# A four-byte read of every later w1 row, placed behind the first x load

## The chip, the core and the metric

The kernel runs on one core of a Trainium2 chip. The metric is the device time of one execution in microseconds, given as the median of several runs. The profile is of one execution, and its times count from the first instruction of its span.

## What is computed

The reference is a two-layer network with a SiLU between, and its gradients:

```
h   = x @ w1            x: 2048 x 640, w1: 640 x 1536
out = silu(h) @ w2      w2: 1536 x 640
(out, dx, dw1, dw2) for the given grad_out, through jax.vjp
```

All tensors are bfloat16. The outputs are out, the gradient of x, that of w1 and that of w2.

## The kernel before

Sizes in the code: S = 2048 rows of x, D = 640, F = 1536, P = 128 partitions, so DT = 5 slices of D and FT = 12 blocks of F. The rows of x are taken in NCH = 4 chunks of SC = 512.

For each chunk the kernel forms h transposed (F on the partitions) from w1 and the transposed x. ScalarE makes the activation aT, ScalarE and VectorE together make its derivative, and g_group (L296 to L308) multiplies that by the gradient that comes back through w2. Two calls of sd_phase (L310 to L328) make the chunk's out and gradient of x. After the four chunks two loops (L398, L425) make the gradients of w2 and of w1.

The first chunk is arranged apart, because nothing is on the chip yet. The names that matter for the change:

- L156 to L160: VectorE fills a 128 x 128 tile, warm, and TensorE multiplies it by itself NWARM = 18 times while the first loads are under way.
- load_x (L182) loads 128 rows of x, 1,280 bytes a row. Block 0 goes out on SP's queue and block 1 on ACT's (L188).
- load_w1 (L185) loads slice k of w1, 128 rows, one to a partition. Slice 0 goes in two halves of columns: columns 0 to 767 on SP, 768 to 1535 on ACT (L189), 1,536 bytes a row each. Slices 1 to 4 go on SP, 3,072 bytes a row (L190 to L192). The tile is w1_nat; the profile's names leave its number out and show it as w_nat, as they do for w2_nat, and show w1 and w2 as in_w_dram.
- L193: SP then transposes the other half of the chunk (rows 256 to 511 of x) on the way in. Behind it on SP's queue stand w2 (L196), the transposed gradient goT (L197, issued at L177), the transposed w2 (L199) and the transposed w1 (L200).
- The list early names the instructions that start_before_entry_wait (L16) moves ahead of the wait at the program's entry: the warm-up, the two x loads, slice 0 and slices 1 and 2. An engine's instructions in that list keep their order.
- pe_x (L202) transposes the first 256 rows of x on TensorE (L208); VectorE and ScalarE copy the result into xT (L213).
- h_first (L268) goes over the slices of w1 first: for each of the 5 slices, 6 pairs of blocks of 256 columns of F are multiplied with the first 256 rows of x (h_pair_mm, L246), two products a pair, so 12 products a slice and 60 in all. Pairs 0 to 2 use the first half of slice 0, pairs 3 to 5 the second half. Then the other 256 rows follow, pair by pair, 60 products more, and sd_phase with w2_nat begins.

[...]Tile contexts put in the semaphore waits. A DMA signals completion on one of eight semaphores, which are used in turn; a DMA that takes a semaphore again waits until its former DMA has landed.

Of the kernel before, what the change touches and what calls it, by code (L numbers as in the profile page):

```python
# [75 lines left out]
def kernel(  # L76
# [11 lines left out]
    nc = tc.nc  # L88
    P = 128
# [8 lines left out]
    ST, DT, FT = S // P, D // P, F // P  # L98
# [11 lines left out]
    dt_in = x.dtype  # L110
# [15 lines left out]
    w1_v = w1.rearrange("(dt p) f -> p dt f", p=P)  # L126
# [19 lines left out]
    with ExitStack() as mctx:  # L146
        cpool = mctx.enter_context(tc.tile_pool(name="cpool", bufs=1))
# [6 lines left out]

        warm = cpool.tile([P, P], dt_in, name="warm")
        early = [nc.vector.memset(warm[:], 1.0)]  # L156
        warm_a = cpool.tile([P, 1], FP32, name="warm_a")
        wp = ps_h.tile([P, SC], FP32, name="wp", tag="hp")
        for i in range(NWARM):
# [22 lines left out]
        def load_x(eng, q):  # L182
            return eng.dma_start(out=x_nat[:, q, :], in_=x_v[:, q, :])  # L183

        def load_w1(k, cols=slice(0, F), eng=nc.sync):  # L185
            return eng.dma_start(out=w1_nat[:, k, cols], in_=w1_v[:, k, cols])

        early += [load_x(nc.sync, 0), load_x(nc.scalar, 1)]  # L188
        early += [load_w1(0, slice(0, F // 2)), load_w1(0, slice(F // 2, F), nc.scalar)]  # L189
        early += [load_w1(k) for k in range(1, 3)]  # L190
        for k in range(3, DT):
# [138 lines left out]
        for c in range(NCH):  # L330
# [15 lines left out]
            if c == 0:  # L346
                h_first(xT, aT, ghT)
                nc.sync.dma_start(
                    out=aT_scr[:, c * SC:(c + 1) * SC].rearrange("(ft p) s -> p ft s", p=P), in_=aT[:]
                )  # L350
                sd_phase(c, w2_nat, aT, oT_scr)
                for ft in range(FT):
                    g_group(ft, goT, ghT)
                nc.sync.dma_start(
                    out=ghT_scr[:, c * SC:(c + 1) * SC].rearrange("(ft p) s -> p ft s", p=P), in_=ghT[:]
# [4 lines left out]
            for i in range(FT + LAG):  # L360
# [7 lines left out]
                out=aT_scr[:, c * SC:(c + 1) * SC].rearrange("(ft p) s -> p ft s", p=P), in_=aT[:]  # L368
            )
            nc.sync.dma_start(  # L370
                out=ghT_scr[:, c * SC:(c + 1) * SC].rearrange("(ft p) s -> p ft s", p=P), in_=ghT[:]
# [7 lines left out]
    with ExitStack() as fctx:  # L379
# [45 lines left out]
        for fc in range(NFC):  # L425
            gh_blk = gh_blks[fc]
            for dt_ in range(DT):
                if dt_ == DT // 2:
                    store_gw2(fc)
                if fc == NFC - 1 and dt_ == DT - 1:  # L430
                    last_stores = []
                    for k, (lo, hi) in enumerate(((0, FC - P), (FC - P, FC))):
# [12 lines left out]
                        else:  # L445
                            nc.vector.tensor_copy(out=g1[:, lo:hi], in_=gp[:, lo:hi])  # L446
                        store = nc.sync.dma_start(
                            out=gw1_v[:, dt_, fc * FC + lo:fc * FC + hi], in_=g1[:, lo:hi]
# [50 lines left out]
```

## Time and profile before

| | us |
|---|---|
| median of 6 runs | 321.42 |
| lowest and highest | 320.25, 322.51 |
| the profiled execution's own time | 322.51 |
| its span, first to last instruction | 320.7 |
| TensorE busy in the span | 315.6 (98%) |
| VectorE busy, ScalarE busy | 102.8, 76.8 |
| bytes moved by DMA | 67.02 MB, 209 GB/s in the mean |

An instruction is shown with the line that made it, its engine, what it writes and reads, and its busy time. An engine name with a q (SPq, ACTq, PEq) is the engine's sequencer, which issues transfers and waits. Matmuls are pipelined: one is shown with its full length from issue to last write, and the distance from one start to the next says what it costs in a row. The time from a DMA's issue to its landing is given apart from the time that its issue takes.

### The profile page before, as it was taken

What the parts mean: (1) busy time and instruction counts of PE and PEld (TensorE: products, weight loads), DVE (VectorE), ACT (ScalarE), POOL (GpSimd) and SP (SyncE); (2) the same over time, 40 slices, a digit from 0 to 9 for tenths busy, and PEclk for the clock granted to TensorE, in tenths of its full rate; (3) what the DMA queues carried; (4) which work ended last, traced back from release to release, by engine and by line L of the source; (5) the groups of instructions that cost most, each with busy time, mean ns of one, the idle gap of its engine ahead of it and who ended that gap; (6) DMA issues with size and microseconds to landing.
All of it is one profiled execution on the core that took longest, in us unless ns stands there. A gap on an engine that the chain in (4) does not pass through costs nothing.

```text
span 320.7 us, 3632 instructions
## 1 busy us (share of the span) xinstructions
PE 315.6 (98%) x1516; PEld 151.7 (47%) x1544; DVE 102.8 (32%) x182; ACT 76.8 (24%) x139; POOL 0.7 (0%) x6
## 2 busy tenths in 40 slices
PE   8999999999999999999999999999999999999997
PEld 6864444444444444444444444444444444444444
DVE  1387450377511077720047751000000110001001
ACT  2392001454211165401145520110100001001010
POOL 0000000000000000000000000000000000000000
PEclk9999999999999999999999999999999999999999
DMA  8999999999969876191636069909999999996111
GB/s 274 302 177 211 211 273 247 325 277 303 293 164 346 213 223 168 57 342 46 174 124 165 0 220 272 246 7 293 213 256 268 243 204 338 243 296 215 47 35 49
DMA packets 147232, 67.02 MB, mean 209 GB/s; under 512 B 113936, under 2 KB 146704, under 8 KB 147216
## 3 DMA queue, kind: packets, MB, share of 16 engines
q1 hardware_dynamic: 146928, 66.43, 82.0%
q10 hardware_dynamic: 288, 0.36, 0.3%
q8 instruction: 12, 0.20, 0.3%
q14 instruction: 4, 0.03, 0.0%
HBM read 9.18 MB, written 28.97 MB: 119 GB/s over the span
## 4 chain that ended last, share of the span: by engine, by line
PE 97%; DMA 2%; issue 1%; ACTq 0%; DVE 0%; DVEq 0%
PE hp L315 32%; PE hp L299 16%; PE hp L404 16%; PE hp L455 15%; PE hp L217 12%; PE hp L246 4%; DMA w_nat<-in_w_dram 2%; PE hp L435 1%; ACTq L183 0%; DVE g L446 0%; DVEq L446 0%; ACTq L483 0%
## 5 line engine op out<-in xcount | busy, mean ns | idle before, releaser
L299 PE MATMUL hp<-goT,w2T 128*128 128x512 bf16 x239 | 56.8, 379 | 0.1
L315 PE MATMUL hp<-ghT,w1T 128*128 128x512 bf16 x235 | 52.2, 379 | 0.3
L315 PE MATMUL hp<-aT,w_nat 128*128 128x512 bf16 x234 | 52.1, 379 | 0.3
L404 PE MATMUL hp<-a_blk,go_nat 128*128 128x512 bf16 x235 | 51.7, 379 | 0.3
L455 PE MATMUL hp<-gh_blk,x_nat 128*128 128x512 bf16 x219 | 48.2, 379 | 0.3
L217 PE MATMUL hp<-xT,w_nat 128*128 128x512 bf16 x174 | 43.4, 379 | 0.3
L323 ACT ACTIVATE oT<-hp 128x512 bf16<-128x512 f32 x24 | 14.5, 604 | 106.8 <-PE hp L315 106.8
L299 PEld LDWEIGHTS <-w2T 128*128 128x128 bf16 x240 | 23.5, 98 | 28.3
L404 PEld LDWEIGHTS <-go_nat 128*128 128x128 bf16 x240 | 23.5, 98 | 28.3
L315 PEld LDWEIGHTS <-w1T 128*128 128x128 bf16 x240 | 23.4, 97 | 28.4
L315 PEld LDWEIGHTS <-w_nat 128*128 128x128 bf16 x240 | 23.5, 98 | 28.1
L306 DVE SCALAR_TENSOR_TENSOR ghT<-ghT,hp 128x512 bf16<-128x512 bf16 x48 | 32.5, 682 | 7.3 <-PE hp L299 7.3
L455 PEld LDWEIGHTS <-x_nat 128*128 128x128 bf16 x224 | 21.9, 98 | 26.4
L325 DVE CAST oT<-hp 128x512 bf16<-128x512 f32 x16 | 11.1, 692 | 72.2 <-PE hp L315 67.7
L226 ACT ACTIVATE aT<-hp 128x512 bf16<-128x512 f32 x36 | 21.5, 597 | 30.4 <-PE hp L217 30.4
L217 PEld LDWEIGHTS <-w_nat 128*128 128x128 bf16 x180 | 17.6, 98 | 21.2
L233 DVE SCALAR_TENSOR_TENSOR ghT<-aT,v 128x512 bf16<-128x512 bf16 x36 | 24.7, 686 | 0.2
L232 DVE TENSOR_SCALAR v<-t 128x512 bf16<-128x512 f32 x36 | 15.4, 427 | 26.7 <-ACT t L230 26.7
L230 ACT ACTIVATE t<-hp 128x512 f32<-128x512 f32 x36 | 21.3, 591 | 0.0
L466 DVE CAST g<-hp 128x512 bf16<-128x512 f32 x7 | 4.8, 692 | 47.0 <-PE hp L455 27.7
L414 DVE CAST g2T<-hp 128x512 bf16<-128x512 f32 x7 | 4.8, 692 | 46.1 <-PE hp L404 46.1
L246 PE MATMUL hp<-xT,w_nat 128*128 128x256 bf16 x120 | 15.9, 301 | 0.6 <-DMA w_nat<-in_w_dram 0.6
(28 smaller groups left out, 68.5 us busy)
## 6 DMA issues: line engine op xcount, KB each, us to landing
aT_scr<-aT SPq DMA_DIRECT2D x4, 1536.0 KB, 6.3
ghT_scr<-ghT SPq DMA_DIRECT2D x4, 1536.0 KB, 8.2
out_dram<-o_sb SPq DMA_DIRECT2D x8, 640.0 KB, 3.3
oT_scr<-oT SPq DMA_DIRECT2D x4, 640.0 KB, 3.6
go_nat<-in_grad_out_dram SPq DMA_DIRECT2D x4, 640.0 KB, 7.4
gxT_scr<-oT SPq DMA_DIRECT2D x4, 640.0 KB, 4.7
w_nat<-in_w_dram SPq DMA_DIRECT2D x1, 1920.0 KB, 11.2
x_nat<-in_x_dram SPq DMA_DIRECT2D x3, 640.0 KB, 7.1
```

Of the source, the lines that this page charges most:

```text
L217: nc.tensor.matmul(hp[:], lhsT=w1_nat[:, dt_, ft * P:(ft + 1) * P], rhs=xT[:, dt_, :], start=(dt_ == 0), stop=(dt_ == DT - 1),)
L226: nc.scalar.activation(aT[:, ft, :], hp[:], ACT.Silu)
L230: nc.scalar.activation(t[:], hp[:], ACT.Tanh, scale=0.5)
L232: nc.vector.tensor_scalar(out=v[:], in0=t[:], scalar1=-0.5, scalar2=0.5, op0=ALU.mult, op1=ALU.add)
L233: nc.vector.scalar_tensor_tensor(out=ghT[:, ft, :], in0=aT[:, ft, :], scalar=1.0, in1=v[:], op0=ALU.subtract, op1=ALU.mult)
L246: nc.tensor.matmul(hp[:, q, :], lhsT=w1_nat[:, dt_, ft * P:(ft + 1) * P], rhs=xT[:, dt_, cols], start=(dt_ == 0 and q == qs[0]), stop=(dt_ ...
L299: nc.tensor.matmul(gp[:], lhsT=w2T[:, dt_, ft * P:(ft + 1) * P], rhs=goT[:, dt_, :], start=(dt_ == 0), stop=(dt_ == DT - 1),)
L306: nc.vector.scalar_tensor_tensor(out=ghT[:, ft, :], in0=ghT[:, ft, :], scalar=1.0, in1=gp[:], op0=ALU.add, op1=ALU.mult)
L315: nc.tensor.matmul(op_[:], lhsT=w_all[:, ft, dt_ * P:(dt_ + 1) * P], rhs=rhs_all[:, ft, :], start=(ft == 0), stop=(ft == FT - 1),)
L323: nc.scalar.activation(oT[:, dt_, :], op_[:], ACT.Copy)
L404: nc.tensor.matmul(gp[:], lhsT=go_nat[:, st, dt_ * P:(dt_ + 1) * P], rhs=a_blk[:, st, :], start=(st == 0), stop=(st == ST - 1),)
L455: nc.tensor.matmul(gp[:], lhsT=x_nat[:, st, dt_ * P:(dt_ + 1) * P], rhs=gh_blk[:, st, :], start=(st == 0), stop=(st == ST - 1),)
```

## The change

A tile of 128 x 4 x 2 elements is added, and one DMA on SP's queue right behind block 0 of x. It reads the first two elements (4 bytes) of each row of w1 in slices 1 to 4: 512 rows, four to a partition. Row p of a slice goes to partition p, as it does in load_w1. The DMA joins the list early. Nothing reads the tile.

```diff
         warm = cpool.tile([P, P], dt_in, name="warm")
         early = [nc.vector.memset(warm[:], 1.0)]
+        touch = cpool.tile([P, DT - 1, 2], dt_in, name="touch")
         warm_a = cpool.tile([P, 1], FP32, name="warm_a")
...
         early += [load_x(nc.sync, 0), load_x(nc.scalar, 1)]
+        early += [nc.sync.dma_start(out=touch[:], in_=w1_v[:, 1:DT, 0:2])]
         early += [load_w1(0, slice(0, F // 2)), load_w1(0, slice(F // 2, F), nc.scalar)]
         early += [load_w1(k) for k in range(1, 3)]
         for k in range(3, DT):
```

## The prediction

> **What bounds the kernel now.** I read the chain that ended last, then the waits of the first 14 us, then the same stretch in order of time.
>
> ```profile
> PE 97%; DMA 2%; issue 1%; ACTq 0%; DVE 0%; DVEq 0%
> PE hp L315 32%; PE hp L299 16%; PE hp L404 16%; PE hp L455 15%; PE hp L217 12%; PE hp L246 4%; DMA w_nat<-in_w_dram 2%; PE hp L435 1%; ACTq L183 0%; DVE g L446 0%; DVEq L446 0%; ACTq L483 0%
> ```
>
> TensorE carries 97% of the chain; the only load on it is w1 (w_nat), 2%. So only the start can move, and a shift there reaches the end one to one if nothing later is waited for. The chain cut to its first 16 us names the load:
>
> ```profile
> 0.63 5.46 DMA w_nat<-in_w_dram
> 6.08 0.04 issue
> 6.13 9.95 PE hp L246 x73
> ```
>
> The transfer issued at 0.63 us (columns 768 to 1535 of slice 0, from ACT) landed at 6.08 and released the products at 6.13. The stretch in order of time (start, length, what, idle before):
>
> ```profile
> 0.54 2.31 SPq L186 DMA_DIRECT2D w_nat<-in_w_dram  x5
> 0.63 0.45 ACTq L186 DMA_DIRECT2D w_nat<-in_w_dram  x1
> 2.84 1.25 PE L208 MATMUL tp<-ident,x_nat 128*128 128x128 bf16 x10 [0.23 <-DMA x_nat<-in_x_dram]
> 3.22 3.67 SPq L193 DMA_TRANSPOSE xT<-in_x_dram  x1
> 3.70 0.85 DVE L213 COPY xT<-tp 128x256 bf16<-128x256 bf16 x2 [3.24 <-PE tp L208]
> 4.04 1.44 PE L246 MATMUL hp<-xT,w_nat 128*128 128x256 bf16 x6
> 6.13 6.13 PE L246 MATMUL hp<-xT,w_nat 128*128 128x256 bf16 x38 [0.65 <-DMA w_nat<-in_w_dram]
> ```
>
> Six products run from 4.04, then TensorE stands for 0.65 us, and from 6.13 it never stops in this stretch. The same products do not always cost the same (stretch, busy, instructions):
>
> ```profile
> 6.13:9.73 3.60, 3.60 (x18) 2.54 (x18) 1.00 1.09 266
> 9.91:13.95 4.04, 4.04 (x39) 3.63 (x37) 1.00 1.10 343
> ```
>
> Their starts lie 213 ns apart until about 9.8 us and 109 ns apart afterwards. The PEclk column prints 1.00 all along; the spacing shows that the array ran at half speed before.
>
> When each slice landed, from the trace's landing records (first of the 16 DMA engines to last, us): slice 0 first half (SP) 3.00 to 3.84; second half (ACT) 3.67 to 6.08; slice 1 4.68 to 6.98; slice 2 5.83 to 7.97; slice 3 7.04 to 8.90; slice 4 9.79 to 9.86. Slice 1 is as late as the half before it: its six products end at 6.13 + 6 x 0.2135 = 7.41, and slice 1 came at 6.98. Some engines trail by about 2 us. The packet records say why: a 3,072-byte row takes 121 ns in the median, but between 3.3 and 5.7 us rows of 1.32 and 1.64 us occur, and some twenty over 0.2 us; later rows hardly ever. This is what a touch could act on.
>
> [...]The profile names no engines, but each w1 landing shows 16 increments. [...]unbroken work from 6.13, full speed at about 9.87, 3.74 us later.[...]
>
> **The change, part by part.**
>
> *SP issue.* One more DMA at 0.54. A 128-row w1 load takes 0.42 us to issue and the next one starts 0.46 after it; w2's 1,536 rows at L196 take 0.58. 512 rows lie between: I take 0.46 (0.42 to 0.65). It pushes slice 0's first half and slices 1 to 4.
>
> *A lane.* The waits of SP show that the ninth DMA waits for an x load before it reuses its semaphore:
>
> ```profile
> SPq L193 <- DMA x_nat<-in_x_dram: 0.3, 1, 0.3
> ```
>
> With one DMA more, the ninth is slice 4, not xT's transpose. It then goes out at about 3.2 instead of 2.43; behind it wait the xT transpose (3.22 to some 3.7), w2_nat and goT. Slice 4 is needed when 48 products have passed: six to 5.27, 18 from 6.13 cold to about 9.9, 24 at 109 ns, 12.5; it landed at 9.86. xT landed at 11.13 and is needed at 13.9, w2_nat at 18.1 against 20.4, goT at 21.4 against 33.5, w1T at 39.8 against 46.5. All have over 2 us of cover against 0.5 to 0.8: price nothing. Were the cover gone, they would cost those 0.5 to 0.8.
>
> *Engine time.* The trace has 9 ns for a 4-byte semaphore packet and 18 ns for a 256-byte packet; 32 of them make 0.29 to 0.58 us on each engine; part of it replaces waiting. I take 0.3. From above: if the touch meets the long waits itself, 1.64 us more (the longest row). From below: if it ends them, a w1 load could land as its first engine did, about 2 us sooner.
>
> *What it removes.* Nothing of the program. The tile is 16 bytes a partition, and nobody reads it, so no consumer waits for it.
>
> *Sum, with the long rows as before.* First half of slice 0: 3.84 + 0.46 + 0.3 = 4.6 instead of in time for 4.04; its six products end at 4.6 + 1.28 = 5.9, inside the pause that lasts to 6.13, which hides them. ACT's half is not behind the touch: 6.1, products to 7.41. Slice 1: 6.98 + 0.76 = 7.74, so 0.3 us of new waiting at 7.41. Slice 2 at 8.7 and later ones find products of 2.56 us a slice ahead of them: no more. Then the clock: the pauses now lie at 3.9 to 4.6 and around 7.5[...]. Each microsecond at 213 instead of 109 ns costs half a microsecond: 0 to 0.8, I take 0.2, since a short pause may be tolerated. Together +0.5 us. The profiled execution took 322.51 us (span 320.7, 1.8 around it) and would become 323.0; it is the slowest of six, so I add the same to the median: 321.42 + 0.5 = **321.9**.
>
> **Rivals.**
>
> *B, the touch works.* [...]For: the long rows begin with slice 1. Against: slices 3 and 4 are first reads too and show few of them, slice 0's first half has none above 0.24 us, and w2's first load from 10.7 us runs at 60 ns a 1,280-byte row with one outlier of 0.33. This looks like a matter of time, not of rows. Worth: first half at 4.6, second by 4.6, slice 1 at 4.68 + 0.76 = 5.4, so products run unbroken from 4.6. Now they are equivalent to unbroken from 6.13 - 1.28 = 4.85: 0.25 gained. [...]In all -1.0 to -2.0, I take -1.4: 320.0.
>
> *C, the wait moves into the touch.* This ends on the slow side. [...]the half slice that the first products need is right behind it. At 1.32 us (one of the two longest rows) it lands at 4.6 + 1.3 = 5.9; the products run from 5.9 where they were equivalent to 4.85: +1.05, and 0.3 for a later full clock: +1.4, 322.8. It decides once that half lands after 4.85 + 0.25, that is with more than half a microsecond of waiting in the touch.[...]
>
> *That it does nothing at all* would need 0 for its slot on SP; I count it to the forecast.
>
> **How the numbers follow.** Forecast 0.40, own range 321.3 to 322.7 (its clock term 0 to 0.8, its shift 0.4 to 1.2); B 0.34, 319.4 to 320.8; C 0.26, 322.4 to 323.8. About 0.3%, 0.96 us, is what a measurement of this kernel can tell from no change. The forecast puts 0.26 within and 0.14 above it, B 0.31 below and 0.03 within, C 0.26 above: faster 0.31, same 0.29, slower 0.40. The range 319.6 to 323.1 cuts the outer ends of B and C.
>
> **What would show it.** In the profile after: an SP issue of about 0.45 us ahead of L186; the first L246 product at 4.5 or later rather than 4.04 (forecast, B); 5.5 or later would be C. An unbroken row of L246 products from there and landings of slice 1 before 6 would be B. The last L246 product now at 20.3 should come at 20.8 by the forecast, 18.9 by B, 21.7 by C. The point where the spacing drops to 109 ns shows the clock's part[...]. I am wrong if rows over 0.2 us vanish, or if the touch's own packets take them over.

## The result and the profile after

The changed kernel takes 321.83 us in the median of 31 runs (319.85 to 322.69), the kernel before 320.66 us in 68 runs (319.78 to 322.51). The ratio is 1.0026, with a 95% interval from 1.0016 to 1.0035: a loss of 0.8 us. That is just under the 0.3% that I had set as the bound, but the interval reaches across it. The ratio goes with the means, which are 0.82 us apart; the medians are 1.17 us apart.

The medians hide the shape. Sorted, the times of the changed kernel fall into two groups with no time between: 9 of 31 lie below 321.0 us (median 320.45), 22 lie above 321.6 (median 322.16). Of the kernel before only 9 of 68 lie above 321.3 (median 321.74, with no gap below them); the other 59 have the median 320.56. So the touch does not make every run slower by 0.8 us. It sends more runs into a late group, which is 1.71 us behind the early one in the changed kernel: 71% instead of 13%. The share of the kernel before is not steady: in three later sets 1 of 44, 7 of 51 and 1 of 27 are late. The profile that the prediction read was of a late run, 322.51 us, the slowest of all 68.

The chain of the changed kernel, from its page; its lines are one to two further down, so slice 0 is L187 and the first products are L248:

```profile
PE 97%; DMA 1%; issue 1%; SPq 0%; DVE 0%; DVEq 0%
```

The chain cut to the first 18 us names another transfer than before (start, length, what):

```profile
0.54 0.41 SPq L190
0.95 0.04 issue
0.99 3.43 DMA w_nat<-in_w_dram
4.42 0.05 issue
4.47 13.58 PE hp L248 x100
```

It was ACT's half of slice 0 that came last; now it is SP's half. The chain leads over the touch's issue (L190), and the products run from 4.47 without the pause that lasted until 6.13. The same stretch in order of time:

```profile
0.54 0.41 SPq L190 DMA_DIRECT2D touch<-in_w_dram  x1
0.62 0.45 ACTq L187 DMA_DIRECT2D w_nat<-in_w_dram  x1
0.99 2.42 SPq L187 DMA_DIRECT2D w_nat<-in_w_dram  x5
2.40 1.31 PE L210 MATMUL tp<-ident,x_nat 128*128 128x128 bf16 x10
3.32 0.85 DVE L215 COPY xT<-tp 128x256 bf16<-128x256 bf16 x2 [2.87 <-PE tp L210]
4.47 7.63 PEld L248 LDWEIGHTS <-w_nat 128*128 128x128 bf16 x48 [1.02 <-DMA w_nat<-in_w_dram]
4.47 7.80 PE L248 MATMUL hp<-xT,w_nat 128*128 128x256 bf16 x47 [0.76 <-DMA w_nat<-in_w_dram]
```

By this profile alone the touch looks like a success: slice 1 had landed by 5.74 instead of 6.98, and nothing is waited for after 4.47. And yet this run took 322.19 us. The reason stands in the pace of the products. Stretch, busy time and count of the L248 products, PEclk, DMA share, GB/s:

```profile
4.50:6.50 2.00, 2.00 (x10) 1.00 0.91 332
6.50:8.50 2.00, 2.00 (x12) 1.00 1.21 363
8.50:9.50 1.00, 1.00 (x6) 1.00 1.06 107
9.70:11.70 2.00, 2.00 (x21) 1.00 1.12 324
```

Up to 9.5 us there are 10 to 12 in two microseconds, from 9.7 on 21. TensorE is "busy" throughout and works at half speed for 5.1 us. (PEclk stays at 1.00 in both; the trace's record of the clock turns to full at 9.61.)

### The profile page after: what moved, and what is told of

It is laid out like the page before. It is cut to its first block, busy times and chain, and to the rows that moved or that the text cites. A ratio compares the mean times of both kernels' runs of the same rounds, so it can differ in the third digit from the quotient of the medians.

```text
span 320.4 us, 3633 instructions
## 1 busy us (share of the span) xinstructions
PE 315.4 (98%) x1516; PEld 151.7 (47%) x1544; DVE 102.8 (32%) x182; ACT 76.8 (24%) x139; POOL 0.7 (0%) x6
## 4 chain that ended last, share of the span: by engine, by line
PE 97%; DMA 1%; issue 1%; SPq 0%; DVE 0%; DVEq 0%
PE hp L317 32%; PE hp L301 16%; PE hp L406 16%; PE hp L457 15%; PE hp L219 12%; PE hp L248 5%; PE hp L437 1%; DMA w_nat<-in_w_dram 1%; SPq L190 0%; SPq L184 0%; DVE g L448 0%; DVEq L448 0%; SPq L485 0%
## 5 line engine op out<-in xcount | busy, mean ns | idle before, releaser
L248 PE MATMUL hp<-xT,w_nat 128*128 128x256 bf16 x120 | 15.8, 302 | 0.8 <-DMA w_nat<-in_w_dram 0.8
```

The source lines that it names most:

```text
L248: nc.tensor.matmul(hp[:, q, :], lhsT=w1_nat[:, dt_, ft * P:(ft + 1) * P], rhs=xT[:, dt_, cols], start=(dt_ == 0 and q == qs[0]), stop=(dt_ ...
```

## The experiments

The theory I began with, the **clock theory**: the touch's place on SP delays slice 0's first half; TensorE therefore pauses longer between the x transposes and the first products; and full speed then comes later. In the profiles of both kernels the products start 213 ns apart up to a point and 109 ns apart behind it (shown 421 and 273 ns long), so about half of the time at half speed is lost. The distance of the two groups, 1.71 us, would be 3.4 us more of it, an estimate. That the pause puts off the turn to full speed was a guess, for the runs to test. (In the second set of the changed kernel, further down, the groups are 2.07 us apart.) Rivals: a **plain delay** by the slot, the **engine time** of the 512 small reads, and that the touch **helps** the later loads while something hides it. "Late" below counts the runs above 321.3 us.

### The kernel before, once more

> The kernel before, once more, for a second profile of its start. Clock theory (the touch holds back slice 0's first half, TensorE pauses longer between the transposes and the first products[...]): the ratio is 1.000; most times lie near 320.5 us and about one in eight near 322, and a profile from the usual group shows full speed from 6 to 8 us on and the last L246 product near 18.6 us, not 20.3. If instead the profile is like the first one while its time lies near 320.5, the clock is not what parts the groups.

Measured: 320.42 us, ratio 0.9994 (0.9984 to 1.0004), none of 14 late; the profiled run 320.53 us. Its products in order of time, then their pace:

```profile
2.63 1.25 PE L208 MATMUL tp<-ident,x_nat 128*128 128x128 bf16 x10
3.84 1.44 PE L246 MATMUL hp<-xT,w_nat 128*128 128x256 bf16 x6
5.71 8.48 PE L246 MATMUL hp<-xT,w_nat 128*128 128x256 bf16 x74 [0.43 <-DMA w_nat<-in_w_dram]
```

```profile
4.50:6.50 2.00, 1.57 (x10) 1.00 0.89 239
6.50:8.50 2.00, 2.00 (x21) 1.00 1.06 397
```

This run, like the first profile, waits for ACT's half (5.66 us) and resumes only at 5.71, while the changed kernel's products have run since 4.47. But the clock is full from 6.22 on, and two microseconds from 6.5 hold 21 products instead of 12. The last L246 product starts at 18.29; in the changed kernel it starts at 19.96, in the first profile at 20.28. A run with the touch's better landings is 1.67 us behind a run with worse ones.

All told, the products of the two runs began equally late: at 3.84 us and 0.64 us of waiting here, at 4.47 without a wait in the changed kernel. What differs is the time at half speed, 1.74 against 5.14 us, and half of that difference is 1.70 us. So in this pair it is the clock that makes the distance, not the landings. The same sum holds in all 14 profiles taken: the last of the first chunk's 120 products starts 12.9 to 13.0 us after the first one's start plus the early waits plus half of the half-speed time. (Seven of the traces have no clock record at the start; there the time at half speed is read from the spacing of the products.)

### The touch behind slice 0's first half

```diff
-        early += [nc.sync.dma_start(out=touch[:], in_=w1_v[:, 1:DT, 0:2])]
         early += [load_w1(0, slice(0, F // 2)), load_w1(0, slice(F // 2, F), nc.scalar)]
+        early += [nc.sync.dma_start(out=touch[:], in_=w1_v[:, 1:DT, 0:2])]
```

> The touch one place later, behind slice 0's first half; slices 1 to 4 still come after it. Clock theory: the first half is back at about 3.9 us, the first products at about 4.05 us, and the ratio falls to between 0.999 and 1.001. Engine-time theory (the 32 reads an engine are the price, wherever they stand): 1.001 to 1.0026. If the touch really shortens the later loads: 0.996 to 0.998, as its help stays and its price goes.

Measured: 320.65 us, 1.0009 (0.9997 to 1.0021), 1 of 13 late. First products at 3.83 us, as expected. A help of the expected size is excluded; a small price of engine time is not. In this profile full speed was there by the first products (12 of them took 1.53 us from 3.83), and those then waited for slice 1, which landed at 6.87:

```profile
PE hp L248 <- DMA w_nat<-in_w_dram: 1.6, 1, 1.6
```

Slices 1 to 3 had been touched before they were loaded, and slice 1 was no earlier for it than in the run above (6.37).

### The slot alone

```diff
-        early += [nc.sync.dma_start(out=touch[:], in_=w1_v[:, 1:DT, 0:2])]
+        early += [nc.sync.dma_start(out=touch[:, 0, :], in_=x_v[:, 0, 0:2])]
```

> A DMA in the touch's place on SP that reads 4 bytes of each row of x's block 0, 128 rows instead of 512, and touches no row of w1. Clock theory: the issue slot of about 0.42 us is what counts, first products at 4.3 to 4.5 us, ratio 1.0015 to 1.003. Engine-time theory: a quarter of the packets, a quarter of the loss, about 1.0007. If the touch helps in part and hides a larger price, this one is slower than the changed kernel: 1.003 to 1.005.

Measured: 321.86 us, 1.0043 (1.0030 to 1.0056), 12 of 15 late. A quarter of the reads, none of them in w1, and no smaller loss: the loss does not go with the number of reads. The products start late here too:

```profile
2.40 1.27 PE L210 MATMUL tp<-ident,x_nat 128*128 128x128 bf16 x10
4.71 5.46 PE L248 MATMUL hp<-xT,w_nat 128*128 128x256 bf16 x30 [1.04 <-DMA w_nat<-in_w_dram]
```

The ratio lies in the band that I had given to "the touch helps in part and hides a larger price". I come back to this with the touch of w2.

### The touch, with TensorE kept busy

```diff
+            for _ in range(8):
+                nc.tensor.matmul(wp[:, 0:P], lhsT=warm[:], rhs=warm[:], start=True, stop=True)
             for k, (tp, (lo, hi)) in enumerate(zip(tps, slices)):
```

> The changed kernel with eight more warm-up products (107 ns each at half speed, 0.85 us) between the x transposes and the first products, in the pause that the touch makes. Clock theory: [...]the late group nearly vanishes, and the ratio falls from 1.0026 to between 0.997 and 1.0003. Plain-delay theory (0.43 us later is 0.43 us longer, no clock in it): the fill runs inside the pause and changes nothing, 1.002 to 1.003.

Measured: 320.38 us, 0.9998 (0.9986 to 1.0011), 1 of 14 late: the whole loss is gone with the touch still in place. The fill did not stand where I wrote it. In the trace the eight products run ahead of the transposes:

```profile
2.40 1.06 PE L214 MATMUL wp<-warm 128*128 128x128 bf16 x8
3.26 1.27 PE L210 MATMUL tp<-ident,x_nat 128*128 128x128 bf16 x10
4.61 5.60 PE L250 MATMUL hp<-xT,w_nat 128*128 128x256 bf16 x44
```

They push the transposes to just before the first products, so the pause closes all the same (0.28 us between the last transpose's 107 ns and 4.61). The products start later than in the changed kernel, and the clock record turns full at 5.92 instead of 9.61. A plain delay can't do that.

### A short pause without a touch

```diff
+        idle_c = cpool.tile([P, HC], dt_in, name="idle_c")
...
+            nc.vector.tensor_copy(out=idle_c[:], in_=tps[0][:].rearrange("p k q s -> p (k q s)"))
             for k, (tp, (lo, hi)) in enumerate(zip(tps, slices)):
```

> The kernel before without any touch; VectorE makes one needless copy of the first transposes (about 0.4 us) ahead of the copy that the first products wait for, so that these start about 0.4 us later while every DMA stays as it was. Clock theory: the pause between transposes and products alone brings the late group back, ratio 1.0015 to 1.0045, more than half of the times above 321.3 us. Rival (the loss comes from what the touch does to the DMA queues and engines): 0.999 to 1.001, since the products are released at 5.7 to 6.1 us by the second half of slice 0 anyway.

Measured: 320.46 us, 0.9996 (0.9974 to 1.0017), 2 of 14 late, beside 7 of 51 of the kernel before. My expectation missed. The copy added only 0.21 us, from one start to the next, not 0.4. In the profiled run it did not even set the start: the first half of slice 0 landed at 4.17 us and released the products.

```profile
4.21 8.04 PE L248 MATMUL hp<-xT,w_nat 128*128 128x256 bf16 x67 [0.19 <-DMA w_nat<-in_w_dram]
```

And the theory as I had put it gave no length for the pause. With a product's slot taken as 107 or 213 ns, TensorE stood between the last transpose and the turn to full speed for 0.80 us in the kernel before once more (full at 6.22) and for 0.39 here (full at about 5.4, an estimate from 12 products in 2.04 us). It stood for 0.97 us in the changed kernel (9.61), 1.02 in the first profile (9.87) and 1.24 with the slot alone (8.89, where the spacing drops). The four profiles taken later with a pause left open have 1.2 to 2.0 us there, and all are of late runs (322.05 to 323.18 us). So in these profiles up to 0.80 us went with an early turn, and 0.97 or more with a late one. Pauses ahead of the transposes are not counted: with them (0.22 us in the kernel before once more, none in the changed kernel) those two would hardly differ. Which pauses matter, and how, is not shown.

### The fill without a touch

The same eight products in the kernel before.

> The kernel before without any touch and with the eight filling products: the first products come some 0.5 to 0.7 us later than in the kernel before, but TensorE doesn't pause. Clock theory: a delay without a pause costs nothing, ratio 0.998 to 1.0005, no late group. Plain-delay theory: 1.0015 to 1.002.

Measured: 320.61 us, 0.9991 (0.9978 to 1.0004), none of 22 late. First products at 4.49 us, as late as in the changed kernel (4.47), with a pause of only 0.16 us in front of them and without a loss:

```profile
3.26 1.27 PE L208 MATMUL tp<-ident,x_nat 128*128 128x128 bf16 x10
4.49 1.29 PE L248 MATMUL hp<-xT,w_nat 128*128 128x256 bf16 x6
5.99 4.21 PE L248 MATMUL hp<-xT,w_nat 128*128 128x256 bf16 x37 [0.21 <-DMA w_nat<-in_w_dram]
```

The wait before 5.99, for ACT's half, came after the clock had turned full at 5.50. Beside the touch with TensorE kept busy this settles it: the same lateness costs with a long pause in front and not without one.

### The touch on ACT's queue

The touch's line goes behind slice 0, with nc.scalar for nc.sync.

> The touch on ACT's queue behind the second half of slice 0: no place on SP's queue ahead of the first half, the same 32 reads an engine at about the time when slice 1 begins. Clock theory: 0.999 to 1.001. Engine-time theory: 1.001 to 1.0026. If the touch shortens the later loads: 0.996 to 0.998.

Measured: 320.52 us, 0.9998 (0.9977 to 1.0019), 4 of 14 late, beside 7 of 51 of the kernel before. All 512 reads are there, and neither a loss nor a gain shows. The interval is wide; a help of 0.3% or more is excluded.

### Longer warm-up

NWARM = 20 and two filling products, no touch.

> The kernel before without any touch, with 20 warm-up products instead of 18 and two more between transposes and first products, so that both short pauses (2.41 to 2.63 us, about 0.2 us behind the transposes) close. Clock theory: full speed comes no later[...], but then the products wait for the slices: 0.998 to 1.000. If the clock doesn't matter: 1.000 to 1.0007, as two to four products are added.

Measured: 320.65 us, 0.9999 (0.9979 to 1.0020), 1 of 14 late. The profiled run had full speed at 4.49 us and then waited twice for slices. No version beats the kernel before. In this profile, with the clock early, it was the slices' landings that held the start back.

### A long pause without a touch, and one meant to be filled

The short pause's copy five times; then the same with ten filling products.

> The kernel before without any touch; five needless copies on VectorE (0.21 us from one to the next) ahead of the copy that the first products wait for, so that these start near 4.9 us and TensorE pauses about 1.2 us behind the transposes, as in the run with the slot alone (1.24 us). [...]Clock theory[...]: ratio 1.0025 to 1.005, most times in the late group near 322 us. Rival (the loss comes from what the added DMA does to queues and engines, and the pause is innocent): 0.999 to 1.0015.

Measured: 322.36 us, 1.0054 (1.0038 to 1.0069), 5 of 6 late. No DMA is added or moved, and the late group is back. The pause was longer than planned, since VectorE made another copy between the needless ones:

```profile
2.81 1.25 PE L209 MATMUL tp<-ident,x_nat 128*128 128x128 bf16 x10 [0.20 <-DMA x_nat<-in_x_dram]
3.67 0.62 DVE L213 COPY idle_c<-tp 128x256 bf16<-128x256 bf16 x2 [3.21 <-PE tp L209]
4.20 0.41 DVE L216 COPY xT<-tp 128x512 bf16<-128x512 bf16 x1
4.53 0.93 DVE L213 COPY idle_c<-tp 128x256 bf16<-128x256 bf16 x3
5.71 6.53 PE L249 MATMUL hp<-xT,w_nat 128*128 128x256 bf16 x45 [1.66 <-DVE xT L216]
```

The pace of the products, in the same form as before:

```profile
5.71:7.71 2.00, 2.00 (x10) 1.00 0.97 364
9.00:11.00 2.00, 2.00 (x21) 1.00 1.15 316
```

The spacing drops at about 8.75 us. Half of the 3.03 us before it, 1.5 us, is lost to half speed. The last L249 product started at 20.16 us; at full speed from 5.71 it would by this estimate have started at about 18.6, not far from the 18.29 of the kernel before once more. So most of the loss is the clock's and the smaller part is the later start.

> As the run with five needless copies, and ten filling products (1.07 us) in the pause: the first products as late, but TensorE busy. Clock theory: 0.999 to 1.001, no late group. If the lateness of the products itself costs, with or without a pause: the same ratio as the run without the filling.

Measured: 323.10 us, 1.0073 (1.0055 to 1.0090), 5 of 6 late. It says nothing about a filled pause: the ten products again ran ahead of the transposes, the needless copies came after these, and the pause stayed:

```profile
2.40 1.27 PE L213 MATMUL wp<-warm 128*128 128x128 bf16 x10
3.47 1.27 PE L209 MATMUL tp<-ident,x_nat 128*128 128x128 bf16 x10
6.41 5.86 PE L251 MATMUL hp<-xT,w_nat 128*128 128x256 bf16 x38 [1.66 <-DVE xT L218]
```

With a pause of 1.9 us and products from 6.41 it shows a late clock and a later start together, no more. That a later start without a pause is harmless therefore rests on the estimate above and on the two runs with eight filling products.

### The same reads in w2, and the changed kernel once more

```diff
-        early += [nc.sync.dma_start(out=touch[:], in_=w1_v[:, 1:DT, 0:2])]
+        early += [nc.sync.dma_start(out=touch[:], in_=w2_v[:, 0:DT - 1, 0:2])]
```

> The touch in its place with the same 512 reads of 4 bytes, but of rows of w2, so that no row of w1 is read early. If the touch's rows do nothing for the later loads: the same as the changed kernel in this call, 1.0015 to 1.0045. If touching w1's rows helps and hides a part of the loss: slower than the changed kernel by 0.001 or more.

> The changed kernel once more, beside the touch of w2 on the same chip. Every theory: 1.0016 to 1.0045, two groups of times, near 320.5 and near 322.1 us, with more than half in the late one.

Measured: 322.28 us, 1.0060 (1.0047 to 1.0073), 5 of 5 late; the changed kernel beside it 322.05 us, 1.0034 (1.0019 to 1.0050), 13 of 22 late. By the difference, 0.0026, touching w1's rows would help. The late groups don't differ, though: median 322.28 against 322.33. What differs is the share, and at the share of both sets of the changed kernel, 35 late of 53, five late runs out of five come up in one case in eight. The landings of slice 1 show no help either: 6.85 with w2 touched, 5.73 with x touched, with w1 touched ahead of it 5.74, 6.53, 6.48 and 6.87, and 5.43 to 6.98 in the seven profiles without a touch. Whether touching w1's rows changes the share a little stays open; with five runs it is not shown.

The profile of the changed kernel once more is again of a late run, 322.32 us, but with another start:

```profile
5.59 6.59 PE L248 MATMUL hp<-xT,w_nat 128*128 128x256 bf16 x45 [1.75 <-DMA w_nat<-in_w_dram]
```

Slice 0's first half landed at 5.55 us instead of 4.43; seven of its rows took over 0.2 us, the longest 0.77. The first products came 1.12 us later than in the first profile of the changed kernel, and the last one only 0.13 us later (20.10 against 19.96), because the spacing dropped at about 8.72 us instead of 9.61. So 4.47 us can't be taken as the touch's usual start, and within the late group an earlier clock can make up for a later start.

## Why the prediction was right, step by step

The forecast was 321.9 us, a shift of 0.5 from a median of 321.42; it came out at 321.83, a shift of 0.8 by the ratio and of 1.17 by the medians. The direction was right, and the time lies in the range of 321.3 to 322.7. That the time was met to 0.1 us is luck: the median of the six runs that I started from was 0.76 us above that of the 68. The mechanism was right in its first half only, up to the later landing of slice 0's first half. Where the loss comes from I had wrong in size: I gave 0.3 us to a wait for slice 1 and 0.2 to the clock, and it was all the clock.

- **The bound.** That only the start can move held: after the start, no new wait of TensorE appeared.
- **SP's issue, 0.46 us.** Measured 0.41 for the issue and 0.455 to the next one's start. Right.
- **Engine time, 0.3 us.** Each read takes 9 ns. 512 of them over the 16 engines are 32 each in the mean, 0.29 us, an estimate; that they spread evenly is not shown. The first of the 16 engines lands slice 0's first half at 3.77 instead of 3.00 us: 0.46 + 0.3. Right as a delay. With the slot alone it is 3.45: only the slot. As a price of its own it doesn't show, since the loss was no smaller with the slot alone.
- **The lane.** The first eight DMAs have eight semaphores in the trace, and the ninth, slice 4, waits on that of x's block 1 (100). It went out at 2.97 us, behind that block's landing at 2.95, and xT's transpose at 3.45. xT landed at 10.71 and covered it. Right: no price.
- **First products at 4.6.** They came at 4.47, and at 5.59 in the other profile. That ACT's half would stay at 6.1, and the pause until then hide the shift, was wrong: it landed at 3.74, and at 3.81 and 3.79 in the two other profiles with the touch in this place. So there was no second pause, and the one in front grew to 0.97 us.
- **0.3 us of waiting for slice 1.** Absent. It was in time at 5.74.
- **The clock, taken at 0.2 out of 0 to 0.8.** This is the term that was mis-sized. I let it grow with the length of the pauses, by at most the time from 6.13 to 7.74. By the times it is a step of 1.71 us: in the profiles full speed came at 6.22 with 0.80 us of pauses and at 9.61, 3.39 us later, with 0.97. The touch raised the share of late runs from 13 to 71%, and 0.58 x 1.71 = 1.0 us, an estimate. The early runs pay nothing by their times: 320.45 against 320.56. So 0.3 + 0.2 stood where 0 + 1.0 belonged, less some tenths within the groups. Why 29% of the runs stay early with the touch in place is not shown, since both profiles of the changed kernel are of late runs.
- **B, the touch works.** The long rows did not vanish. In single profiles, rows of 3,072 bytes over 0.2 us numbered 22 to 29 in the seven without a touch, 25, 29, 23 and 27 with w1 touched ahead, 24 with x and 16 with w2 touched instead. The longest fell from 1.64 and 1.75 us to between 0.83 and 1.19, but with x touched it was 1.05, with w2 touched 1.47 and with a short pause and no touch at all 0.68. No effect of the rows read shows. The 1.0 to 2.0 us that I gave B were an estimate, and no run shows them.
- **C, the wait moves into the touch.** None of its packets took over 9 ns, in any of the profiles. False. The sign that I had named for it, first products at 5.5 or later, did appear in the second profile of the changed kernel (5.59), but there it was long rows of slice 0 itself. Nor does a stall show at the end of ACT's half in the first profile: its last six packets take 65 ns each and start 0.18 to 0.21 us apart (4.66 to 5.59), near the sum of one 3,072-byte row (0.121) and one 1,536-byte row (0.065). The 1.4 us that I gave C were an estimate.
- **The profile that I read.** I added the shift to the median, as if the profiled run stood for it. That run turned to full speed as late as 9.87 us and so could not show the price that most runs would pay.

## What to carry to other kernels

When a small change at a kernel's start moves the median, look at the sorted times first: two groups with a gap between them say that something is lost whole or not at all, and such an edit is priced by the share of runs that it sends across. Delay is not the same as idleness here: first products some 0.6 us later cost nothing with TensorE kept busy, and 1.7 us in most runs with a pause of 1 us in front of them. Before warming anything by reads, test the slot alone.

## What was not expected of the hardware

With 0.80 us of pauses between the last transpose and the turn, full speed came at 6.22 us; with 0.97, only at 9.61. The trace's clock record, in the seven profiles that have one at the start, turned full anywhere between 4.49 and 9.87 us. Rows of 3,072 bytes that take 0.2 to 1.75 us instead of 0.12 occur at the start of every profile taken, with w1 touched or not; their cause was not looked for. And in the first profile 17 of the 256-byte packets of x's DMA transpose, begun from 8.1 us on, took 0.29 to 1.61 us, where 18 ns is the median, and ended together at 9.69 to 9.73, after the last row of w1 (9.48). Why they did is not shown.
